# Sharing a ninth pair of attention weights, with a new order of steps in the second chunk and three roundings moved to ScalarE

## The chip, the core and the metric

The kernel runs on one core of a Trainium2 chip. The metric is the device time of one execution in microseconds (us); of several executions the median is given. The engines are TensorE (PE in the profile; PEld is its weight load), VectorE (DVE), ScalarE (ACT), GpSimd (POOL) and SyncE (SP), which issues most DMAs.

## The reference

Two stages are computed. The first is an attention without softmax, for 8 batches of 2496 tokens with keys and queries from the same array z (64 wide) and values v (256 wide):

```python
scores = scale * np.matmul(z, z.transpose(0, 2, 1))
attn = np.maximum(scores, 0.0) ** 2
out = np.matmul(attn, v)
return (u * out).astype(np.float32)
```

The second is a mixture of 8 experts over the 19968 rows that come out: a gate picks the expert of each row, a skip score leaves some rows as they are, and each expert is relu(x w1) w2. The weights attn are symmetric, since queries and keys are the same z: the weight of query i on key j is that of query j on key i. The change touches the attention stage alone.

## The kernel before, in words

**Tiling.** A batch's queries are cut into five chunks c = 0 to 4 (the first four of 512 queries, the fifth of 448). The keys are cut into ten steps p = 0 to 9 of 256 keys; steps 2j and 2j+1 cover the tokens of chunk j. All 40 chunks of the 8 batches follow one another in one written order, 400 steps in all. `ORDER[c]` says in which order a chunk takes its ten steps; a place in that order is called a position, 0 to 9. The first chunk of the first batch goes in plain order.

**A step's weights.** All products are made in three parts, from high and low halves of float32 numbers: the tile `ah` is the weight rounded to the float32r type, `al` is what is left. `scores` (line 263) makes six matmuls into PSUM (two run side by side on half the rows of the array, so they come in three pairs). ScalarE applies Relu (line 304) and Square (line 305) into a tile `r`. Line 327 rounds `r` to `ah`, on ScalarE or on VectorE as `on_act` says. VectorE subtracts to get `al` (line 331).

**Shared weights.** For a pair (i, j) of `PAIRS`, chunk i computes the weights of its steps 2j and 2j+1 and keeps them: `keep` (line 280) transposes each with two VectorE instructions into a tile `rt`, and after both steps four DMAs put it into DRAM (`kept`, line 292 reads it and line 705 issues the puts). Chunk j later does not compute its steps 2i and 2i+1 but recalls them, with four DMAs a step (`recall`). A recalled step has no scores, no Relu and no Square. In the fifth chunk, which is narrower, a recalled step is rounded and subtracted in three pieces. In the first batch the pairs with chunk 0 are not used.

**Where roundings run.** `on_act` gives a step's rounding to ScalarE if the step belongs to a pair or stands in `EXTRA[c]`, to VectorE otherwise.

**The order of one step s** (the loop over `steps`, `k` is the position). First `ahead` issues the recall of step s + 5 on SP. Then `stage` prepares the weights of step s + 2: scores, Relu, Square, rounding, subtraction, and the transposes of `keep`. Then `attend` multiplies the weights of step s with the values: 12 matmuls for each half d of the 256 outputs (line 358). Within the 12, the ninth is the first that needs `al`. At position 0 only d = 0 is done; at position 1 d = 0, then d = 1 of positions 0 and 1; at position 8 only d = 0; at position 9 d = 0, then d = 1 of positions 8 and 9. Then come the step's other jobs, by the table `todo`: loads of the next batch's z and v and their roundings, the transposed result rows (`rows0`, `rows1`, line 395), stores, and, during every second chunk, the routing of the last two chunks (`gates` on TensorE at position 1; `route`, `counts` on VectorE at position 3; `place` at position 5). Last, `put_some` issues up to four waiting puts on SP.

**The end of a chunk.** At position 9 the sums leave PSUM: `part(0, 1)` is a copy on ScalarE (line 386) and `part(0, 0)` an addition on VectorE (line 388), both after d = 0; `part(1, 1)` and `part(1, 0)` come after d = 1. The rounding and subtraction of the next chunk's position 0 are held back to here:

```python
high, low = rest
if s + 1 < len(steps) and not on_act(*steps[s + 1]):
    high()
    low()
    high = low = lambda: None
part(0, 1, acc[0])
part(0, 0, acc[0])
high()
low()
high, low = stage(s + LA)
```

So a rounding on VectorE comes before the copies, one on ScalarE behind the first copy. The rounding of the next chunk's position 1, if that step is not recalled, stands behind the copy `part(1, 1)` of the chunk's last sums, and its subtraction behind the chunk's last addition, `part(1, 0)`. Every engine runs its instructions in the written order.

**Buffers.** Two PSUM tiles for scores, five tiles `r` (recalls and computed steps share them), three each of `ah` and `al`, two of `rt`.

Of the kernel before, what the change touches and what calls it, by code (L numbers as in the profile page):

```python
# [25 lines left out]

PAIRS = ((0, 1), (0, 2), (0, 3), (1, 2), (1, 3), (2, 3), (2, 4), (3, 4))
ORDER = (  # L30
# [5 lines left out]
)  # L36
EXTRA = ((8,), (3, 8), (4, 5), (6, 7), (1, 3))


C_TRI, C_REV, C_OFF, C_IDS, C_THR, C_END = 0, 128, 192, 256, 260, 270  # L40
# [7 lines left out]
def attn_moe(ctx, tc, zT, uT, v, wg, w1, w2, cst, pad, out):  # L48
# [168 lines left out]
    def pairs(b):  # L217

        return PAIRS if b else [x for x in PAIRS if x[0]]

# [4 lines left out]
    def on_act(ci, p):  # L225
        b, c = ci // NQ, ci % NQ
        j = p // 2
        if (b, c) == (0, 0):
            return p in (4, 6)
        return (j, c) in pairs(b) or (c, j) in pairs(b) or p in EXTRA[c]  # L230

    kept = {x: dram.tile([QC, QC], F32, name="kept%d%d" % x) for x in PAIRS}
    HALF = (slice(0, 64), slice(64, 128))
# [796 lines left out]
```

## Time and profile before

| what | value |
|---|---|
| time, median of 3 runs (lowest, highest) | 1773.52 us (1771.78, 1775.19) |
| the profiled execution: its time, its span | 1774.26 us, 1772.5 us |
| TensorE matmuls | busy 1751.5 us, 99% of the span |
| TensorE weight loads | busy 1571.7 us, 89% |
| VectorE | busy 1196.0 us, 67% |
| ScalarE | busy 1159.2 us, 65% |
| DMA | 267.47 MB, mean 151 GB/s |

The span runs from the first to the last instruction; the time of an execution contains some 1.8 us around it. Matmuls overlap in the records, so a TensorE that is busy all the time need not be at its peak: what shows its pace is the distance from one matmul's start to the next. The attention stage ends at about 1275 us; the experts follow.

### The profile page before, as it was taken

To read this page: it belongs to the slowest core of one execution; us is meant where nothing else is said; L and a number is where in the kernel's file an instruction comes from. 1 tells how busy PE (TensorE), PEld (TensorE's weight loads), DVE (VectorE), ACT (ScalarE), POOL (GpSimd) and SP (SyncE) were. 2 spreads that over 40 slices of the span, in tenths; PEclk is the share of its full clock that TensorE was granted. 3 is DMA by queue.
4 is the path that set the end of the run, shared out by engine and by line. 5 is a ranking of instruction groups with operands and counts; after the bars stand their busy time and mean duration, and the time that the engine had idled before them with its cause. 6 is when DMAs were issued, how large, how long until landed. Compare 5 with 4: busy or idle time off the path is not lost. (4 is left out here: it accounts for less than half of the span.)

```text
span 1772.5 us, 40706 instructions
## 1 busy us (share of the span) xinstructions
PE 1751.5 (99%) x15844; PEld 1571.7 (89%) x15844; DVE 1196.0 (67%) x2113; ACT 1159.2 (65%) x1499; POOL 491.4 (28%) x483
## 2 busy tenths in 40 slices
PE   8999999999999999999999999999999999999998
PEld 6879888988888898888889888888899999999998
DVE  6878877887887787788778778867753333343332
ACT  8878877887788788778778877877533323333321
POOL 1102212211220221221122022112355546635721
PEclk9999999999999999999999999999999999999999
DMA  5576689478858947885794789579543323323210
GB/s 191 126 186 147 162 212 226 103 197 219 175 141 203 226 108 195 219 201 134 185 219 114 195 211 206 119 193 217 146 112 88 82 80 110 92 54 93 87 38 27
DMA packets 403766, 267.47 MB, mean 151 GB/s; under 512 B 205859, under 2 KB 334117, under 8 KB 403440
## 3 DMA queue, kind: packets, MB, share of 16 engines
q1 hardware_dynamic: 389440, 240.47, 55.6%
q0 software_dynamic: 13712, 22.99, 4.6%
q8 instruction: 142, 2.33, 0.6%
q14 instruction: 184, 1.51, 0.3%
q10 hardware_dynamic: 288, 0.17, 0.0%
HBM read 145.80 MB, written 118.39 MB: 149 GB/s over the span
## 5 line engine op out<-in xcount | busy, mean ns | idle before, releaser
L358 PE MATMUL acc<-ah,vh 64*128 64x512 f32 (+1 forms) x3120 | 654.6, 383 | 1.2 <-DVE ah L327 0.6
L358 PE MATMUL acc<-ah,vl 64*128 64x512 f32 (+1 forms) x3120 | 638.0, 382 | 0.0
L331 DVE TENSOR_TENSOR al<-r,ah 128x1024 fp32r<-128x1024 f32 (+3 forms) x464 | 488.4, 1068 | 185.2 <-ACT ah L327 175.4
L358 PE MATMUL acc<-al,vh 64*128 64x512 f32 (+1 forms) x3120 | 506.3, 383 | 2.2 <-DVE al L331 1.6
L517 POOL DMA_INDIRECT lst<-pair,dest x160 | 197.2, 1233 | 911.7 <-DVE dest L515 875.9
L304 ACT ACTIVATE r<-ps 128x1024 f32<-128x1024 f32 (+1 forms) x278 | 279.9, 1007 | 167.7 <-PE ps L263 158.7
L358 PEld LDWEIGHTS acc<-ah,vh 64*128 64x128 f32 x3120 | 344.6, 184 | 50.7 <-ACT ah L327 3.5
L358 PEld LDWEIGHTS acc<-ah,vl 64*128 64x128 f32 x3120 | 343.3, 184 | 41.3 <-DVE vl L120 0.3
L358 PEld LDWEIGHTS acc<-al,vh 64*128 64x128 f32 x3120 | 320.5, 184 | 53.0 <-DVE al L331 11.7
L327 ACT CAST ah<-r 128x1024 fp32r<-128x1024 f32 (+3 forms) x381 | 330.6, 892 | 55.5 <-PE acc L358 35.4
L305 ACT ACTIVATE r<-r 128x1024 f32<-128x1024 f32 (+1 forms) x278 | 290.0, 1043 | 8.8
L622 ACT ACTIVATE hh<-psh 128x512 fp32r<-128x512 f32 (+1 forms) x172 | 99.1, 584 | 287.9 <-PE psh L617 249.4
L617 PE MATMUL psh<-xt,w1h 128*128 128x256 f32 (+1 forms) x1280 | 235.3, 285 | 2.0 <-ACT xt L588 1.4
L636 PE MATMUL y<-w2t,hh 128*128 128x256 f32 x1328 | 235.5, 280 | 0.0
L623 DVE SCALAR_TENSOR_TENSOR hl<-psh,hh 128x512 fp32r<-128x512 f32 (+1 forms) x172 | 113.3, 671 | 137.5 <-ACT hh L622 134.6
L636 PEld LDWEIGHTS y<-w2t,hh 128*128 128x128 f32 x1328 | 201.8, 188 | 1.0 <-issue 0.6
L617 PEld LDWEIGHTS psh<-xt,w1h 128*128 128x128 f32 x1280 | 197.4, 189 | 2.9 <-issue 2.9
L636 PE MATMUL y<-w2t,hl 128*128 128x256 f32 x664 | 184.5, 278 | 1.3 <-DVE hl L623 1.3
L617 PE MATMUL psh<-xt,w1l 128*128 128x256 f32 (+1 forms) x640 | 182.1, 285 | 0.5 <-issue 0.5
L280 DVE STREAM_TRANSPOSE rt<-r 128x512 f32<-128x512 f32 x244 | 158.3, 686 | 0.7 <-DMA kept<-rt 0.5
L636 PEld LDWEIGHTS y<-w2t,hl 128*128 128x128 f32 x664 | 124.7, 188 | 1.7 <-DVE hl L623 1.7
L666 POOL DMA_INDIRECT out<-o,idt x77 | 76.7, 996 | 171.4 <-DVE o L665 148.6
(178 smaller groups left out, 1694.9 us busy)
## 6 DMA issues: line engine op xcount, KB each, us to landing
kept<-rt SPq DMA_DIRECT2D x244, 256.0 KB, 4.7
r<-kept SPq DMA_DIRECT2D x488, 128.0 KB, 4.5
raw<-in_v SPq DMA_DIRECT2D x80, 256.0 KB, 4.4
ut<-in_uT SPq DMA_DIRECT2D x32, 512.0 KB, 4.6
xr<-xrow SPq DMA_DIRECT2D x128, 128.0 KB, 3.2
out<-xrow SPq DMA_DIRECT2D x128, 128.0 KB, 3.0
raw<-in_w SPq DMA_DIRECT2D x64, 256.0 KB, 3.7
zf<-in_zT SPq DMA_DIRECT2D x40, 256.0 KB, 4.9
```

The lines of the kernel that those rows point to most:

```text
L280: nc.vector.transpose(t[:, :, 32 * k : 32 * k + 32], r[:, x, :].rearrange("p (m i) -> p m i", i=32))
L304: nc.scalar.activation(r[:, :, :n], ps[:, :, :n], AF.Relu, scale=isc)
L305: nc.scalar.activation(r[:, :, :n], r[:, :, :n], AF.Square)
L327: (nc.scalar.copy if on_act(ci, p) else nc.vector.tensor_copy)(h_, r_)
L331: nc.vector.tensor_sub(l_, r_, f32(h_))
L358: nc.tensor.matmul(acc[t][:, :n], w[h, x, dd], a[h, x, :n], start=(first and t not in halves[:m]), stop=(last and t not in halves[m + 1 :]),)
L517: put = nc.gpsimd.indirect_dma_start(out=lst, out_offset=bass.IndirectOffsetOnAxis(ap=dest[:, t : t + 1], axis=0), in_=pair[:, t, :], in_o ...
L617: nc.tensor.matmul(ps[:, j * W : (j + 1) * W], wt[:, a, o : o + P], x[:, d, :W], start=(m == 0), stop=(m == 5),)
L622: nc.scalar.activation(hh[:, : G * W], ps[:, : G * W], AF.Relu)
L623: nc.vector.scalar_tensor_tensor(hl[:, : G * W], ps[:, : G * W], 0.0, f32(hh[:, : G * W]), op0=ALU.max, op1=ALU.subtract)
L636: nc.tensor.matmul(ys[t], h[:, tt], w2t[f][:, k, :], start=(f == 0 and m == 0 and t % 2 == 0), stop=(f == NF - 1 and m == 2), skip_group_c ...
L666: put = nc.gpsimd.indirect_dma_start(out=out, out_offset=bass.IndirectOffsetOnAxis(ap=ids[:, t, 0:1], axis=0), in_=ot, in_offset=None, bou ...
```

## The change

A ninth pair, (1, 4), is added: the second chunk keeps its weights of steps 8 and 9, and the fifth chunk recalls its steps 2 and 3 from them. The second chunk takes its steps in a new order. `EXTRA` changes for the second and the fifth chunk. In the second chunk step 8 leaves the list, but as part of a pair it stays on ScalarE, and step 9 joins it there. In the fifth chunk steps 0, 2 and 8 move from VectorE to ScalarE (steps 0 and 8 by the list, step 2 as part of the pair), steps 1 and 3 stay on ScalarE, and only step 9 is left on VectorE.

```diff
-PAIRS = ((0, 1), (0, 2), (0, 3), (1, 2), (1, 3), (2, 3), (2, 4), (3, 4))
+PAIRS = ((0, 1), (0, 2), (0, 3), (1, 2), (1, 3), (1, 4), (2, 3), (2, 4), (3, 4))
 ORDER = (
     (0, 1, 2, 3, 8, 4, 5, 6, 7, 9),
-    (2, 3, 0, 4, 1, 5, 8, 6, 7, 9),
+    (2, 4, 5, 0, 6, 7, 1, 8, 9, 3),
     (4, 0, 1, 6, 2, 7, 3, 8, 9, 5),
     (6, 0, 2, 1, 8, 3, 9, 4, 5, 7),
     (0, 1, 2, 3, 4, 5, 6, 7, 8, 9),
 )
-EXTRA = ((8,), (3, 8), (4, 5), (6, 7), (1, 3))
+EXTRA = ((8,), (3,), (4, 5), (6, 7), (0, 1, 8))
```

In the new order of the second chunk, steps 0 and 1 are recalled at positions 3 and 6 (before: 2 and 4). Steps 4 to 9 are kept, at positions 1, 2, 4, 5, 7 and 8 (before: steps 4 to 7 at positions 3, 5, 7 and 8).

## The prediction

> **What bounds the kernel now.** First the page's busy times, then the chunks one by one, then the borders instruction by instruction.
>
> ```profile
> span 1772.5 us, 40706 instructions
> PE 1751.5 (99%) x15844; PEld 1571.7 (89%) x15844; DVE 1196.0 (67%) x2113; ACT 1159.2 (65%) x1499; POOL 491.4 (28%) x483
> PEclk9999999999999999999999999999999999999999
> ```
>
> TensorE is busy throughout at full clock. Busy time by windows, of the fifth batch: the second chunk (with a routing in it), the fourth, the fifth (without), and the fourth batch's fifth (with) (columns: window, length, busy PE, PEld, DVE, ACT, POOL with counts, clock, DMA share, GB/s).
>
> ```profile
> 677.35:710.44 33.09, 33.09 (x315) 27.01 (x313) 26.92 (x56) 26.82 (x31) 4.05 (x4) 1.00 0.76 185
> 741.24:774.19 32.95, 32.63 (x306) 26.24 (x308) 26.57 (x52) 22.87 (x28) 5.28 (x4) 1.00 0.89 225
> 774.19:801.78 27.59, 27.59 (x272) 25.70 (x270) 23.25 (x36) 21.77 (x35) 6.33 (x8) 1.00 0.73 157
> 615.67:644.69 29.02, 29.02 (x308) 27.65 (x306) 26.00 (x61) 21.94 (x37) 4.85 (x4) 1.00 0.66 156
> ```
>
> Every chunk is TensorE's: matmul time removed shortens it, unless a weight comes late and TensorE stands. ScalarE and VectorE are 70% to 90% busy, so whether one comes late is settled at places, not on the average. The place that decides is the border from fourth to fifth chunk (fifth batch; timeline of ScalarE, VectorE, TensorE):
>
> ```profile
> 771.99 0.95 ACT L305 ACTIVATE r<-r 128x896 f32<-128x896 f32 x1
> 773.79 0.59 ACT L386 COPY xrow<-acc 128x512 f32<-128x512 f32 x1 [0.84 <-PE acc L358]
> 774.27 0.94 ACT L327 CAST ah<-r 128x896 fp32r<-128x896 f32 x1
> 774.41 0.69 DVE L388 TENSOR_TENSOR xrow<-acc,xrow 128x512 f32<-128x512 f32 x1 [1.79 <-ACT xrow L386]
> 775.25 1.09 DVE L331 TENSOR_TENSOR al<-r,ah 128x896 fp32r<-128x896 f32 x1 [0.15 <-ACT ah L327]
> 773.13 0.62 PE L358 MATMUL acc<-al,vh 64*128 64x512 f32 x4
> 773.58 0.36 PE L263 MATMUL ps<-zh 64*128 64x448 f32 x2
> 774.19 0.36 PE L358 MATMUL acc<-ah,vh 64*128 64x448 f32 x2
> 775.00 0.57 PE L358 MATMUL acc<-al,vh 64*128 64x448 f32 x4
> 775.41 0.36 PE L263 MATMUL ps<-zh 64*128 64x448 f32 x2
> 776.02 0.36 PE L358 MATMUL acc<-ah,vh 64*128 64x448 f32 x2
> 776.82 0.57 PE L358 MATMUL acc<-al,vh 64*128 64x448 f32 x4
> ```
>
> The old chunk's last matmul issues before 773.58; its sums are copied from 773.79; behind the copy position 1's rounding runs to 775.21 and its subtraction to 776.34. TensorE meanwhile does step 2's scores (773.58 to 774.19), position 0 (to 775.41), step 3's scores (to 776.02), and starts position 1 at 776.02, needing `al` at 776.82. Both arrive in time, by 0.81 and 0.48 us.
>
> **The change part by part.** *Scores removed.* The two sets of scores just named are what the ninth pair takes away: 0.61 us each (774.19 - 773.58; 776.02 - 775.41), 1.22 us a batch, 9.8 us over eight. They are also the cover of that rounding.
>
> *What the cover hid.* Without them position 0 starts at 773.58 and is through after 1.22 us (775.41 - 774.19), at 774.80. The copy cannot start earlier, as the last sums are no earlier; so `ah` still ends at 775.21, `al` at 776.34. (Position 0's rounding now also sits on ScalarE behind the first copy and pushes the Relu and Square by 0.94 us, but the Square, which ended at 772.94, then ends near 773.8, when the copy starts anyway.) What a late weight costs TensorE, the border of the fourth chunk shows already:
>
> ```profile
> 740.14 2.00 ACT L327 CAST ah<-r 128x1024 fp32r<-128x1024 f32 x2
> 741.22 2.36 DVE L331 TENSOR_TENSOR al<-r,ah 128x1024 fp32r<-128x1024 f32 x2 [0.26 <-ACT ah L327]
> 741.24 0.50 PE L358 MATMUL acc<-ah,vh 64*128 64x512 f32 x2
> 741.58 0.39 PE L358 MATMUL acc<-ah,vl 64*128 64x512 f32 x2
> 742.50 0.73 PE L358 MATMUL acc<-al,vh 64*128 64x512 f32 x4
> ```
>
> TensorE starts 0.05 us after the first of the two casts ends (741.19), 0.05 us again after the subtraction that ends at 742.45 (the first of two, 1.23 us), and after each stand the next pair comes 0.11 us later than usual (0.34 us instead of 0.23; four matmuls of `al` in 0.73 us instead of the 0.62 of the row at 773.13). So in the changed fifth chunk position 1 starts at 775.26, 0.46 us late; its `al` is wanted 0.80 us on (776.82 - 776.02), at 776.06, and usable at 776.39: 0.33 more; restarts 2 x 0.11. Together 1.0 us. The fifth chunk gains 1.22 - 1.0 = 0.2 us, 1.6 us over eight batches. Bounds of the stall: nothing, if that rounding gets ahead of the copy, up to the whole 1.22.
>
> *Rest of the fifth chunk.* ScalarE loses two Relus and two Squares, VectorE three roundings; recalled steps pay more for their pieces. From position 2 on each step is recalled as positions 4 to 7 are now, and these run without a stand (27.59 us busy of 27.59), so I charge nothing; the cover is TensorE's 2.43 us a step (twice 1.22).
>
> *Second chunk.* Its count of computed and recalled steps is unchanged, so TensorE's work is. VectorE gets four transposes more and one rounding less.
>
> ```profile
> L280 DVE STREAM_TRANSPOSE rt<-r 128x512 f32<-128x512 f32 x244 | 158.3, 686 | 0.7 <-DMA kept<-rt 0.5
> L327 DVE CAST ah<-r 128x1024 fp32r<-128x1024 f32 x51 | 36.6, 718 | 17.7 <-ACT r L305 17.5
> ```
>
> 4 x 0.686 - 0.718 = 2.0 us more in 33.09, of which 26.92 are busy. ScalarE gets that rounding. It fits on average; the tight place is position 6 where a routing runs (VectorE, then TensorE, batch 5):
>
> ```profile
> 691.90 1.23 DVE L331 TENSOR_TENSOR al<-r,ah 128x1024 fp32r<-128x1024 f32 x1 [2.84 <-ACT ah L327]
> 693.05 1.30 DVE L280 STREAM_TRANSPOSE rt<-r 128x512 f32<-128x512 f32 x2
> 694.27 0.18 DVE L459 TENSOR_REDUCE mx<-lg 128x8 f32<-128x64 f32 x1
> 697.69 0.69 DVE L120 TENSOR_TENSOR vl<-raw,vh 128x512 fp32r<-128x512 f32 x1
> 698.29 2.35 DVE L331 TENSOR_TENSOR al<-r,ah 128x1024 fp32r<-128x1024 f32 x2
> 698.84 0.40 PE L358 MATMUL acc<-ah,vh 64*128 64x512 f32 x2
> 699.76 0.62 PE L358 MATMUL acc<-al,vh 64*128 64x512 f32 x4
> ```
>
> From 691.90 VectorE runs without a gap: position 5's subtraction, its transposes, the routing, the load's remainder, then position 6's subtraction, which ends near 699.5, a quarter of a microsecond before the 699.76 at which TensorE wants it. Scores for position k + 2 run at the start of position k: up to position 6 that is at positions 1, 3, 4, 5, 6 in the old order, at 0, 2, 3, 5, 6 in the new. So position 5's scores, made at position 3, stand behind two sets instead of one, and its Relu with the whole train behind it comes one set, 0.68 us, later (three pairs, each half of 773.58 - 773.13). Position 6 stands behind five sets either way: its need is no later, and it is now the recalled step 1. VectorE's gap of 2.84 us ahead of the train takes up the transposes that moved before it. `al` comes near 700.2, 0.45 us late, plus 0.11 to restart: 0.56 us. Chunks alternate, so four of eight second chunks have a routing: 2.2 us. Without the routing's 3.4 us (694.27 to 697.69) nothing is late. Bounds: 0 if the train's slack is larger than I read, 1.0 us a chunk if the added transposes of positions 1 and 2 push it too.
>
> *DMAs.* The pair adds four puts, which wait on SP for VectorE's transposes with recalls and stores behind them; the second chunk's DMA share is 0.76, and the puts of steps 4 to 7 now go out earlier, so I charge nothing. The moved recalls are wanted later than before. It adds eight recalls of 128 KB, 1.05 MB, to the busiest stretch:
>
> ```profile
> 768.75 2.46 SPq L292 DMA_DIRECT2D r<-kept  x4
> 779.34 2.98 SPq L292 DMA_DIRECT2D r<-kept  x4
> 777.00:780.00 3.00, 3.00 (x32) 2.78 (x32) 2.35 (x5) 2.94 (x5) 1.87 (x2) 1.00 1.05 240
> r<-kept SPq DMA_DIRECT2D x488, 128.0 KB, 4.5
> 793.04 0.37 PE L358 MATMUL acc<-ah,vh 64*128 64x448 f32 x2
> L331 DVE TENSOR_TENSOR al<-r,ah 128x384 fp32r<-128x384 f32 x64 | 39.5, 657 | 2.5 <-ACT ah L327 2.4
> ```
>
> The new ones stand on SP just ahead of the first row. The last old one is issued by 782.3 and lands 4.5 us on, at 786.8; position 7, which uses it, starts at 793.04 and wants `al` 0.8 us later, with at most 3 us for the pieces' rounding and subtraction before: the data has until 790.8, 4.0 us of slack. 1.05 MB at 240 GB/s is 4.4 us if DMA engines, at a share of 1.05 here, give everything back one to one. SP is ahead of TensorE, so I take part of it as hidden, cost 0; the other bound is 0.6 us a batch and more if transfers lengthen.
>
> By the Trainium skill's "Perfetto Trace Analysis", section Identifying the Most-Contended Engine, a DMA share misleads and use of the HBM is to be read instead; with the roughly 358 GB/s limit of "DMA: Bandwidth & Descriptors", section Specifications, 240 leaves room, 1.05 MB would be an estimated 2.9 us, inside the slack. No run here shows that rate; the trace has shares of 1.0 at 240.
>
> *The sum.* -9.8 + 8 x 1.0 + 2.2 = +0.4 us on the profiled execution's 1774.26, so 1774.7. That execution lies 0.7 us above the median shown, 1773.52: on the median 1773.9, and I predict 1774.
>
> **The rivals.**
>
> *The cover isn't needed: faster.* If position 1's rounding is not what TensorE waits for in the fifth chunk, the 8.0 us of stalls are saved: 1774 - 8 = 1766. For: today both arrive with 0.5 us to spare. Against: copy, rounding and subtraction follow one another, whatever else is removed.
>
> *The recalls come late: slower.* A full DMA stretch delays the fifth chunk's last recalls. It decides above 4.0 us of delay; at 4.8 us, 0.8 us a batch, 6.4 us in all: 1780. For: the share above 1. Against: only the last two recalls are near their limit.
>
> *TensorE has room: no change, a little slower.* The weight loads fill 25.70 of the fifth chunk's 27.59 us; if the remaining 1.89 us were idle time, 1.22 us of removed scores would buy nothing and only the second chunk's 2.2 us stay: 1776. Against: matmul pairs start every 0.20 us (775.00 to 775.41 for two), without a gap. The skill's section named above judges TensorE's headroom by weight loads and would read it so; this trace's even spacing speaks against it.
>
> *The change doesn't do what it says.* All three roundings do leave VectorE (0, 2 and 8), and the recalled steps exist; no weight on this.
>
> **How the numbers follow.** Forecast 0.53, faster rival 0.23, late recalls 0.19, room on TensorE 0.05. The forecast's own range is 1770.5 to 1777. From the rivals the range goes to 1765.5 and 1780, which leaves about 0.15 out. This kernel's measurement tells 0.2%, 3.5 us, from no change. Faster by more: 0.24 (the first rival, and a sliver of the forecast). Slower by more: 0.20 (late recalls, a sliver likewise). Within: 0.56.
>
> **What would show it.** In the fifth chunk: twelve score matmuls fewer, and a stand of TensorE at position 1 of about 1 us, released by ScalarE's `ah` and VectorE's `al`; the chunk 0.2 us shorter. If it is 1.2 us shorter, the cover was not needed. In second chunks with routing: a stand at position 6 near 0.5 us, released by `al`. If ScalarE waits for `r` from DMA there, the late recalls hold. A stall at a place not named here would make the prediction wrong as worked.

## The result, and the profile after

The changed kernel takes 1802.03 us (median of 4 runs, 1800.55 to 1807.37); the kernel before, run beside it, 1774.3 us. The ratio is 1.0167, with an interval of 1.0155 to 1.0179: slower by 30 us by the ratio, where 1774 us (no change) was forecast. The profiled execution is the slowest of the four (1807.37 us), so sums over its trace come out some 5 us larger than the medians would give. The page after, busy times and one row of its DMA issues (count, size, median us to landing):

```profile
span 1805.5 us, 40756 instructions
PE 1761.0 (98%) x15748; PEld 1541.1 (85%) x15748; DVE 1199.2 (66%) x2145; ACT 1161.5 (64%) x1531; POOL 503.7 (28%) x483
r<-kept SPq DMA_DIRECT2D x552, 128.0 KB, 4.8
```

96 matmuls fewer (15844 before), 64 recalls more (488 before): the change does what it says. The same windows as in the prediction (fourth batch's fifth chunk with a routing; of the fifth batch the second, the fourth and the fifth):

```profile
628.40:662.90 34.50, 30.55 (x303) 25.32 (x300) 25.36 (x63) 21.18 (x40) 5.46 (x4) 1.00 0.77 187
696.22:729.13 32.91, 32.58 (x308) 26.05 (x306) 28.34 (x59) 27.24 (x31) 5.30 (x4) 1.00 0.82 203
760.23:792.56 32.33, 32.02 (x301) 25.51 (x302) 26.01 (x51) 23.02 (x28) 5.94 (x4) 1.00 0.90 215
792.56:823.96 31.40, 29.32 (x267) 24.44 (x264) 22.34 (x38) 20.76 (x38) 7.56 (x9) 1.00 0.81 187
```

The second and fourth chunks are a little shorter in these windows. (A window begins at the chunk's first product with values; a set of scores of the second chunk falls into the first chunk's window now, and the fourth chunk's has lost one of the two sets that the pair removes.) The fifth chunks are where the time goes: 29.02 to 34.50 us and 27.59 to 31.40 us, though each has a set of scores less. TensorE is idle for 2.1 us of the last row's 31.40 (31.40 - 29.32); in the prediction's rows the fifth chunks had no idle time. The DMA engines are as full as they were: over the first 20 us of this chunk, in which the recalls land, their share is 0.99 at 230 GB/s, where the same stretch before (774.19 to 794.19) has 1.00 at 216.

The predicted stand at the border is there. Timeline of the fifth batch's border (start, us, engine, instruction, idle time and its releaser):

```profile
792.76 0.59 ACT L386 COPY xrow<-acc 128x512 f32<-128x512 f32 x1
793.25 0.94 ACT L327 CAST ah<-r 128x896 fp32r<-128x896 f32 x1
794.22 1.09 DVE L331 TENSOR_TENSOR al<-r,ah 128x896 fp32r<-128x896 f32 x1
794.24 0.47 PE L358 MATMUL acc<-ah,vh 64*128 64x448 f32 x2 [0.31 <-ACT ah L327]
795.37 0.67 PE L358 MATMUL acc<-al,vh 64*128 64x448 f32 x4
```

Position 1's first pair starts 0.67 us after the pair ahead (0.20 is the pace), the first pair of `al` 0.42 us after its own, and the pair behind each comes another 0.11 us late: about 0.9 us together. But this is the smaller part. Adding up over the eight fifth chunks by how much the distance from one pair's start to the next is above 0.20 us gives 7.0 us at position 1, 10.5 us at positions 2 to 7, 3.5 us at position 8 and 13.4 us at position 9. (At the end of two of these chunks TensorE ran at half its clock for 3.41 us, as the last section shows; the wider spacing there is about 1.5 us of the sum at position 8.) The waits of ScalarE, first in the kernel before, then after (what waits, for what: us in total, times, longest), name the cause:

```profile
ACT ah L327 <- DMA r<-kept: 6.7, 7, 3.4
```

```profile
ACT ah L327 <- DMA r<-kept: 73.7, 44, 3.0
```

ScalarE waits for recalled weights, 44 times instead of 7. Timeline of SP in the fifth chunk of the fifth batch (DMAs issued; a row ends when the last of them is issued):

```profile
793.50 3.09 SPq L292 DMA_DIRECT2D r<-kept  x4
796.85 0.35 SPq L103 DMA_DIRECT2D zf<-in_zT  x1
797.30 2.50 SPq L292 DMA_DIRECT2D r<-kept  x4
800.09 0.35 SPq L95 DMA_DIRECT2D raw<-in_v  x1
800.63 2.53 SPq L292 DMA_DIRECT2D r<-kept  x4
803.54 0.35 SPq L103 DMA_DIRECT2D zf<-in_zT  x1
804.03 3.04 SPq L292 DMA_DIRECT2D r<-kept  x4
807.12 0.43 SPq L95 DMA_DIRECT2D raw<-in_v  x1
```

SP goes from one issue to the next almost without a break. From 793.50 to 804.03 it needs 10.5 us for three steps of four recalls and a load: 3.5 us a step, 0.70 us a DMA. TensorE asks for a step every 2.43 us. The issues themselves take only 5.1 of the 10.5 us (0.30 to 0.42 us each); the rest is waiting between them. What SP waits for while it issues recalls, before and after:

```profile
SPq L292 <- DVE al L331: 21.3, 16, 2.8
SPq L292 <- DMA r<-kept: 11.1, 14, 1.9
```

```profile
SPq L292 <- DMA r<-kept: 21.9, 51, 2.5
SPq L292 <- DMA raw<-in_v: 14.9, 18, 2.7
```

Before, its longest wait was for VectorE to free a tile `r`, the sign of a queue that is ahead; after, that wait is down to 2.1 us. All its waits at recalls for DMAs to land come to 36 us before and 58 us after. SP's DMAs go through eight semaphores in turn: of the 693 DMAs in the trace of after that have a record of their landing, none was followed, eight DMAs later, by one issued before that landing, and 128 by one issued within 0.15 us of it (50 of 484 before). Eight in flight at the 4.8 us of the page's row is one every 0.6 us.

Last, what the late recall does to ScalarE and TensorE (same chunk):

```profile
811.41 1.13 ACT L327 CAST ah<-r 128x384 fp32r<-128x384 f32 x3 [1.76 <-DMA r<-kept]
812.96 0.91 ACT L304 ACTIVATE r<-ps 128x896 f32<-128x896 f32 x1
816.26 0.91 ACT L304 ACTIVATE r<-ps 128x896 f32<-128x896 f32 x1
```

```profile
818.87 0.47 PE L358 MATMUL acc<-ah,vh 64*128 64x448 f32 x2 [1.19 <-DVE ah L327]
820.06 0.67 PE L358 MATMUL acc<-al,vh 64*128 64x448 f32 x3 [0.32 <-DVE al L331]
```

ScalarE stands until 811.41 for step 7's recall. The Relus of steps 8 and 9 are behind that rounding on ScalarE, so they come late too, and TensorE has its longest stand of this chunk, 1.19 us, at position 9, whose weights are computed and not recalled.

### The profile page after: what moved, and what is told of

The parts are those of the page before. It is cut to its first block, busy times and chain, and to the rows that moved or that the text cites. A ratio compares the mean times of both kernels' runs of the same rounds, so it can differ in the third digit from the quotient of the medians.

```text
span 1805.5 us, 40756 instructions
## 1 busy us (share of the span) xinstructions
PE 1761.0 (98%) x15748; PEld 1541.1 (85%) x15748; DVE 1199.2 (66%) x2145; ACT 1161.5 (64%) x1531; POOL 503.7 (28%) x483
## 4 chain that ended last, share of the span: by engine, by line
PE 65%; DMA 14%; ACT 8%; DVE 6%; SPq 3%; issue 3%; POOL 0%; DVEq 0%; POOLq 0%; ACTq 0%
PE acc L358 35%; PE psh L617 11%; PE y L636 10%; PE ps L263 7%; DMA r<-kept 7%; DVE al L331 3%; ACT ah L327 2%; ACT r L305 2%; SPq L292 2%; ACT r L304 2%; DMA out<-o,idt 2%; DMA zf<-in_zT 2%; DMA xr<-xrow 1%; DMA raw<-in_v 1%; DVE rt L280 1%
## 5 line engine op out<-in xcount | busy, mean ns | idle before, releaser
L358 PE MATMUL acc<-ah,vh 64*128 64x512 f32 (+1 forms) x3120 | 638.1, 386 | 15.4 <-DVE ah L327 7.7
L358 PE MATMUL acc<-ah,vl 64*128 64x512 f32 (+1 forms) x3120 | 620.3, 382 | 0.0
L358 PE MATMUL acc<-al,vh 64*128 64x512 f32 (+1 forms) x3120 | 495.1, 386 | 8.3 <-DVE al L331 7.0
L327 ACT CAST ah<-r 128x1024 fp32r<-128x1024 f32 (+3 forms) x445 | 364.4, 847 | 126.6 <-DMA r<-kept 73.7
L358 PEld LDWEIGHTS acc<-ah,vh 64*128 64x128 f32 x3120 | 319.2, 184 | 79.7 <-ACT ah L327 18.6
L358 PEld LDWEIGHTS acc<-al,vh 64*128 64x128 f32 x3120 | 301.6, 184 | 74.7 <-DVE al L331 29.0
L358 PEld LDWEIGHTS acc<-ah,vl 64*128 64x128 f32 x3120 | 319.3, 185 | 46.4 <-DVE vl L120 0.3
L304 ACT ACTIVATE r<-ps 128x1024 f32<-128x1024 f32 (+1 forms) x262 | 265.3, 1012 | 131.1 <-PE ps L263 122.8
L305 ACT ACTIVATE r<-r 128x1024 f32<-128x1024 f32 (+1 forms) x262 | 274.7, 1049 | 8.3
L280 DVE STREAM_TRANSPOSE rt<-r 128x512 f32<-128x512 f32 x276 | 179.1, 687 | 0.6 <-DMA kept<-rt 0.5
```

The lines of the kernel that those rows point to most:

```text
L280: nc.vector.transpose(t[:, :, 32 * k : 32 * k + 32], r[:, x, :].rearrange("p (m i) -> p m i", i=32))
L304: nc.scalar.activation(r[:, :, :n], ps[:, :, :n], AF.Relu, scale=isc)
L305: nc.scalar.activation(r[:, :, :n], r[:, :, :n], AF.Square)
L327: (nc.scalar.copy if on_act(ci, p) else nc.vector.tensor_copy)(h_, r_)
L358: nc.tensor.matmul(acc[t][:, :n], w[h, x, dd], a[h, x, :n], start=(first and t not in halves[:m]), stop=(last and t not in halves[m + 1 :]),)
```

## The experiments

Theory: the recalls come late because SP can't issue them fast enough, having only eight DMAs in flight (the program's eight semaphores). Rivals: the added bytes (DMA engines or memory full); the border's order; the roundings on ScalarE; the new order of the second chunk. Every ratio is against the kernel before, run beside the experiment, since the kernel before itself took between 1773 and 1787 us from one chip to another; a time in an expectation is to be read as its ratio to 1774.

**The parts without the ninth pair.** `e1_order`: the kernel before with the new order of the second chunk. `e2_round`: the kernel before with the fifth chunk's roundings of the kernel after.

```diff
-    (2, 3, 0, 4, 1, 5, 8, 6, 7, 9),
+    (2, 4, 5, 0, 6, 7, 1, 8, 9, 3),
```

```diff
-EXTRA = ((8,), (3, 8), (4, 5), (6, 7), (1, 3))
+EXTRA = ((8,), (3, 8), (4, 5), (6, 7), (0, 1, 2, 3, 8))
```

Expected of `e1_order`:

> The kernel before with the new order of the second chunk alone (no ninth pair, the roundings as before). By the prediction's step: one late subtraction at position 6 in four chunks, 0.56 us each: 1776 to 1777. If the order costs nothing: 1774. If the order is what costs: above 1785.

Expected of `e2_round`:

> The kernel before with the fifth chunk's steps 0, 2 and 8 rounded on ScalarE, as in the change, and nothing else. Late recalls (theory): no recall is late, the roundings have cover, 1773 to 1777. Rival, the roundings on ScalarE cost: above 1785.

Measured: 1.0018 (1.0009 to 1.0028) and 1.0010 (0.9998 to 1.0022): 3 us and 2 us, so neither part explains the 30. As far as the parts add up, the pair itself brings the rest.

**More DMAs on the kernel before.** Eight extra DRAM-to-DRAM DMAs a batch at the place of the new recalls, of 128 KB (`e9_bytes`) or of 4 KB (`e10_slots`). Nothing uses what they write.

```diff
+            if ci % NQ == 4 and p in (2, 3):
+                d = dram.tile([8, 32, 2, QC], F32, name="dum%d" % s)
+                src = kept[2, 4].rearrange("(a k i) q -> a i k q", a=4, k=4)
+                for a in range(4):
+                    nc.sync.dma_start(d[4 * (p - 2) + a], src[a, :, p % 2 * 2 : p % 2 * 2 + 2, :])
```

(`e10_slots` takes `:16` of the last dimension on both sides.)

Expected of `e9_bytes`:

> The kernel before with eight DMAs more a batch, at the places in SP's order where the change puts the eight new recalls: 128 KB each, from the kept weights to an unused place in DRAM; nobody waits for them and nothing else is changed, the scores are still made. Late recalls: the four old recalled steps now come late by about 4 to 5 us less the 4.0 us of slack and the 1.2 us that the scores still take, so 1775 to 1790, with ScalarE waiting for r from DMA. Rivals (roundings, order, lost cover): 1774.

Expected of `e10_slots`:

> As the run with eight extra DMAs of 128 KB, but of 4 KB each (64-byte runs): they take places among SP's eight in flight but hardly any bytes. If places are what is short, it costs at least half of what the 128 KB ones cost; if bytes, nothing: 1774.

Measured: 1.0117 (1.010 to 1.0134) and 1.0108 (1.0085 to 1.013). A thirty-second of the bytes, nearly the same time. ScalarE's wait in each:

```profile
ACT ah L327 <- DMA r<-kept: 62.5, 33, 4.1
```

```profile
ACT ah L327 <- DMA r<-kept: 45.3, 26, 3.7
```

And SP with the 4 KB DMAs:

```profile
778.26 6.31 SPq L714 DMA_DIRECT2D dum<-kept  x8
```

0.79 us for each 4 KB: the bytes don't count here. (A DMA of 4 KB has as many separate runs, 64, as one of 128 KB, so the number of runs is left as a rival; `e17_one` below, with the runs of a step unchanged, settles it.) With no scores taken away, the kernel before loses some 20 us to eight DMAs a batch.

**The same bytes in fewer DMAs.** `e6_two` recalls a step with two DMAs of 256 KB over all 128 partitions; the DRAM side's outermost step is the four blocks `a`.

```diff
-        src = kept[p // 2, ci % NQ].rearrange("(a k i) q -> a i k q", a=4, k=4)
-        for a in range(4):
-            nc.sync.dma_start(r[32 * a : 32 * a + 32], src[a, :, p % 2 * 2 : p % 2 * 2 + 2, :])
+        src = kept[p // 2, ci % NQ].rearrange("(a k i) q -> k a i q", a=4, k=4)
+        for x in range(2):
+            nc.sync.dma_start(r[:, x, :], src[p % 2 * 2 + x])
```

Expected of `e6_two`:

> The changed kernel with every recall made by two DMAs of 256 KB instead of four of 128 KB; the bytes are the same. If the recalls are late because SP has no more than eight DMAs in flight (each DMA waits for the one eight before it): half as many places taken by recalls, 1774 to 1785. If they are late because the DMA engines are full of bytes: unchanged, 1797 to 1806, the 256 KB landing about twice as late as the 128 KB (9 us instead of 4.8).

Measured: 1.1912, ScalarE waiting for recalls nearly everywhere:

```profile
ACT ah L327 <- DMA r<-kept: 463.8, 156, 6.3
```

That is far from any answer of the expectation. By the Trainium skill's "DMA: Bandwidth & Descriptors", section Why a DMA increments its semaphore by 16 and not by 1, a DMA uses the largest number of engines, up to 16, that divides the slowest dimension of both sides, here 4; no view shows the engines one by one, so the cause isn't shown, and the run says nothing on the number of DMAs.

`e17_one` therefore changes the layout in DRAM: `keep` writes its 32-row blocks in another order, so that the 128 partitions of a recall are evenly spaced, and one DMA of 512 KB brings a step.

```diff
-            nc.vector.transpose(t[:, :, 32 * k : 32 * k + 32], r[:, x, :].rearrange("p (m i) -> p m i", i=32))
+            nc.vector.transpose(
+                t[:, :, 32 * k : 32 * k + 32].rearrange("p (k a) i -> p k a i", k=4),
+                r[:, x, :].rearrange("p (a k i) -> p k a i", a=4, k=4),
+            )
...
-        for a in range(4):
-            nc.sync.dma_start(r[32 * a : 32 * a + 32], src[a, :, p % 2 * 2 : p % 2 * 2 + 2, :])
+        src = kept[p // 2, ci % NQ].rearrange("(k e) q -> e k q", k=4)
+        nc.sync.dma_start(r, src[:, p % 2 * 2 : p % 2 * 2 + 2, :])
```

Expected of `e17_one`:

> The changed kernel with the kept weights laid out in DRAM so that a recalled step comes with one DMA of 512 KB instead of four of 128 KB; the bytes are the same. If the number of DMAs in flight (eight from SP, each about 5 us) is what delays the recalls, the fifth chunk's late recalls go and only the stand at its position 1 (1.0 us) is left: ratio 0.999 to 1.004. If the bytes (DMA engines or HBM full at 240 GB/s) delay them, the recalls stay late and the ratio stays at 1.012 to 1.018.

Measured: 1.0006 (0.9997 to 1.0016). Its page, its fifth chunk of the fifth batch, ScalarE's wait, and SP's largest wait at the recalls (line 294 here):

```profile
r<-kept SPq DMA_DIRECT2D x138, 512.0 KB, 6.6
```

```profile
775.70:803.57 27.87, 27.51 (x266) 24.81 (x264) 22.14 (x38) 20.87 (x38) 7.70 (x8) 1.00 0.68 184
```

```profile
ACT ah L329 <- DMA r<-kept: 0.7, 1, 0.7
```

```profile
SPq L294 <- DVE al L333: 63.6, 38, 3.5
```

Each DMA takes longer to land (6.6 us against 4.8) and moves four times as much. A step still consists of 256 runs of 2 KB. The chunk moves its bytes at 184 GB/s, as in the slow kernel (187), and its first 20 us at 256 GB/s against 230; yet no recall of a fifth chunk is late, and SP is ahead again: it waits for free tiles, and at the recalls not once for a landing. TensorE has one stand left, the one at position 1:

```profile
777.38 0.47 PE L360 MATMUL acc<-ah,vh 64*128 64x448 f32 x2 [0.31 <-ACT ah L329]
```

With `e9_bytes` and `e10_slots`: neither the bytes nor the number of runs is the cause, but the number of DMAs; and the late recalls cost 1.0167 - 1.0006, or 1.6%: 28.5 us, 3.6 us a batch, good to some 3 us by the two intervals. `e20_b_one` gives the kernel before the same recall:

Expected of `e20_b_one`:

> The kernel before (eight pairs, its own order and roundings), with one DMA of 512 KB a recalled step. In the kernel before no recall comes late at a fifth chunk, so if late recalls are all that the DMAs cost, it gains nothing: ratio 0.998 to 1.002. If fewer DMAs make the kernel faster in themselves, it comes to 0.997 or below, and the gain of the ninth pair with one DMA a step is not the pair's.

Measured: 1.001 (1.0001 to 1.002), as expected. It gains nothing where nothing was late.

**Other ways around the lateness.** `e5_late`: the kernel after, with the last six loads of the next batch begun behind the recalls.

```diff
-            jobs += [(load_v, 7, 4, 2), (load_z, 2, 4, 3), (load_v, 8, 4, 4), (load_z, 3, 4, 5)]
-            jobs += [(load_v, 9, 4, 6), (load_z, 4, 4, 7)]
+            jobs += [(load_z, 4, 4, 8), (load_v, 8, 4, 9), (load_z, 2, 4, 10), (load_v, 7, 4, 11)]
+            jobs += [(load_z, 3, 4, 12), (load_v, 9, 4, 13)]
```

Expected of `e5_late`:

> The changed kernel with the last six loads of the next batch (z and v) begun some four to six steps later, behind the fifth chunk's recalls. Late recalls: the recalls no longer share the queue with them and land in time; of the 33 us that fifth chunks grew by, only the stand at position 1 stays (about 1.0 us a batch), so 1774 to 1782. Rivals that lay it to the roundings, the order or the lost cover alone: unchanged within 4 us, 1798 to 1806.

Measured: 1.0068 (1.0051 to 1.0084), more than the 1.000 to 1.005 expected. The fifth chunks keep little but the stand at position 1 (7.1 us over the eight, and 1.5 us at positions 3 and 4 of three of them), and the first chunks, into which the loads' casts move, become 0.7 us longer each, which I hadn't priced. In the kernel after, too, the last fifth chunk, with no next batch to load, stands for 1.1 us by the sum above, the other seven for 3.8 to 5.5. Loads and recalls share SP's eight places, so fewer loads among the recalls help them as fewer DMAs a recall do.

`e3_dve`: the kernel after with steps 0 and 8 of the fifth chunk rounded on VectorE (`EXTRA[4]` is `(1,)`).

Expected of `e3_dve`:

> The changed kernel with the fifth chunk's steps 0 and 8 rounded on VectorE again. Late recalls (theory): the fifth chunk's recalls still land late, since no DMA is changed; only the knock-on at position 9 shrinks, because ScalarE has 0.94 us less to do between the late step 7 and step 9's Relu. At most 0.9 us a batch, so 1795 to 1801 us. Rival, the roundings on ScalarE are what costs: back to 1775 to 1780.

Measured: 1.0133 (1.0115 to 1.015), some 6 us less than the kernel after and within what was expected. The recalls stay as late (ScalarE waits 43 times for them, 87.9 us), but the stand at position 9 shrinks, from 1.19 to 0.46 us in the fifth batch:

```profile
808.73 0.47 PE L358 MATMUL acc<-ah,vh 64*128 64x448 f32 x2 [0.46 <-DVE ah L327]
```

Over all fifth chunks the sum at position 9 falls from 13.4 to 9.3 us. This is the part that passes through ScalarE's order: one rounding less ahead of step 9's Relu.

`e11_pool` issues the recalls of steps 2 and 3 from GpSimd's queue instead of SP's.

```diff
+            eng = nc.gpsimd if ci % NQ == 4 and p in (2, 3) else nc.sync
-            nc.sync.dma_start(r[32 * a : 32 * a + 32], src[a, :, p % 2 * 2 : p % 2 * 2 + 2, :])
+            eng.dma_start(r[32 * a : 32 * a + 32], src[a, :, p % 2 * 2 : p % 2 * 2 + 2, :])
```

Expected of `e11_pool`:

> The changed kernel with the eight new recalls (the fifth chunk's steps 2 and 3) issued on GpSimd's queue instead of SP's; bytes, times and readers are the same. If SP's places in flight are what is short, SP's queue is as it was before: only the stand at position 1 stays, 1774 to 1782. If bytes are short: unchanged, 1797 to 1806.

Measured: 1.0197 (1.018 to 1.0214), slower still, as neither answer had it. The fifth batch's step 3, and the clock behind it:

```profile
789.58 2.25 POOL L293 DMA_DIRECT2D r<-kept  x4
800.08 2.15 ACT L328 CAST ah<-r 128x384 fp32r<-128x384 f32 x6 [5.93 <-DMA r<-kept]
801.26 0.65 PE L359 MATMUL acc<-ah,vh 64*128 64x448 f32 x2 [4.35 <-ACT ah L328]
```

```profile
801.26:804.50 3.24, 3.24 (x18) 2.95 (x20) 3.24 (x9) 3.03 (x8) 1.99 (x2) 0.52 1.06 234
```

These recalls, all issued by 791.83, had landed only when ScalarE could start at 800.08, so the run doesn't test the places on SP. After the stand of 4.35 us TensorE ran at a granted clock of 0.52.

**The border.** `e18_swap`: the kernel after with steps 1 and 2 of the fifth chunk exchanged, so that a recalled step, whose rounding can run ahead of the copy, is at position 1. `e15_swap_late` adds the late loads of `e5_late`, `e19_swap_one` instead the recall of `e17_one`. `e7_inter` goes further and puts computed steps among all the recalled ones.

```diff
-    (0, 1, 2, 3, 4, 5, 6, 7, 8, 9),
+    (0, 2, 1, 3, 4, 5, 6, 7, 8, 9),
```

`e7_inter` has `(0, 2, 1, 3, 8, 4, 5, 9, 6, 7)` there.

Expected of `e18_swap`:

> The changed kernel with the exchange of steps 1 and 2 in the fifth chunk alone. The stand at position 1 goes, the recalls stay late: both theories expect 1.0167 less 0.45%, 1.010 to 1.014. If it falls to 1.000 or below, the stand at position 1 was what made the recalls late.

Expected of `e15_swap_late`:

> The changed kernel with four DMAs a recall, the exchange of steps 1 and 2 in the fifth chunk, and the last six loads of the next batch moved behind the recalls. The late loads alone left the stand of 1.0 us in the fifth chunk and 0.7 us more in the first chunk, ratio 1.007. The exchange takes the 1.0 us away: eight times, 8 us, 0.45%: ratio 1.001 to 1.004.

Expected of `e19_swap_one` ("the one above" is `e17_one`):

> The one above, and in the fifth chunk step 2 (recalled) at position 1 and step 1 (computed) at position 2. The copy of the last sums then no longer stands ahead of position 1's rounding, so that the 1.0 us stand goes too: the 9.8 us of removed scores stay, less 2.2 us at the second chunk: ratio 0.995 to 0.998 if the number of DMAs is the cause, 1.008 to 1.014 if the bytes are.

Expected of `e7_inter`:

> The changed kernel with the fifth chunk in the order 0, 2, 1, 3, 8, 4, 5, 9, 6, 7: the six recalled steps are spread over nine positions and one of them sits at position 1. The DMAs are the same in number and bytes over the chunk. Late recalls because six in a row ask for 24 DMAs faster than SP's eight places give them: mostly cured, and the stand at position 1 (1.0 us a batch) with it, 1766 to 1778. If the DMA engines lack bandwidth over the chunk: 1790 or more.

Measured: `e18_swap` 1.0178 (1.0161 to 1.0195), no better than the kernel after, against my expectation. `e15_swap_late` 1.0017 (1.0005 to 1.0029), `e19_swap_one` 0.9971 (0.9961 to 0.9982), `e7_inter` 1.0072 (1.0046 to 1.0097), where 0.996 to 1.002 was expected. In the trace of `e18_swap` the stand at position 1 is gone, but the recalls are as late as after (ScalarE waits 43 times for them, 78.5 us): with late recalls the time is the same; that the wait has only moved is argued. Where they aren't late it gains 0.5% (`e5_late` to `e15_swap_late`) and 0.35% (`e17_one` to `e19_swap_one`), 6 to 9 us, near the 8.0 us that I gave position 1. The computed steps among the recalled ones (`e7_inter`) give SP time, so that ScalarE waits less for recalls than after, but not all of the lateness goes:

```profile
ACT ah L327 <- DMA r<-kept: 51.5, 28, 6.5
```

The fifth chunk of `e19_swap_one` runs without a stand, 0.61 us shorter than before (27.59):

```profile
771.15:798.13 26.98, 26.98 (x266) 24.97 (x264) 21.62 (x37) 21.36 (x36) 6.23 (x8) 1.00 0.63 175
```

`e13_inter_pool` joins `e7_inter` and `e11_pool`:

Expected of `e13_inter_pool`:

> Both: the spread order of the fifth chunk and the eight new recalls on GpSimd's queue. If late recalls and the stand at position 1 are the whole loss, what is left is 9.8 us of scores saved less 2.2 us in the second chunk: 1766, at most 1772. If something else costs too: above 1775.

Measured: 1.0233 (1.0216 to 1.025). ScalarE waits up to 9.0 us for a recall; with the recalls from GpSimd's queue as late as that, this run too tells nothing of SP.

**The second chunk.** `e4_oldorder` is the kernel after with the old order of the second chunk, `e12_pairorder` one with `(2, 3, 0, 4, 1, 5, 6, 7, 8, 9)`. Both steps of a pair are turned into the one tile `rt` of the chunk, one after the other. In `e4_oldorder` steps 8 and 9 stand around 6 and 7. In `e12_pairorder` the written order is right, but the kernel puts off the transposes of position 8 until behind those of position 9 (lines 334 and 789), so that step 9's come before step 8's. In both, the kept weights are a mixture of steps of two pairs: this part of the computation is changed.

Expected of `e4_oldorder`:

> The changed kernel with the old order of the second chunk (the ninth pair and the roundings stay). Late recalls: the new order costs only its stand at position 6 in the four second chunks with a routing, 0.56 us each, so about 2 us less, 1798 to 1801. Rival, the new order upsets the second chunk and what follows: under 1785.

Expected of `e12_pairorder`:

> The changed kernel with the second chunk in the order 2, 3, 0, 4, 1, 5, 6, 7, 8, 9: the old one, with step 8 moved behind 7, so that the two kept steps 8 and 9 follow one another as the ninth pair's tile needs. Late recalls: this takes away only the stand at position 6 in routed second chunks, 0.56 us in four chunks: 1798 to 1802. If the new order is to blame: under 1785.

Measured: 1.0278 (1.026 to 1.0297) and 1.0273 (1.0251 to 1.0295), outside both answers. Since the dependencies of the transposes and puts change with it, neither says what the order costs; `e1_order` does.

`e21_swap_one_load` is `e19_swap_one` with one load begun a position later, so that its remainder on VectorE (line 120) is no longer ahead of position 6's subtraction.

```diff
-            jobs = [(load_v, 0, 1, 3), (load_z, 0, 1, 6), (load_v, 1, 2, 3), (load_z, 1, 2, 5), (load_v, 2, 2, 7)]
+            jobs = [(load_v, 0, 1, 4), (load_z, 0, 1, 6), (load_v, 1, 2, 3), (load_z, 1, 2, 5), (load_v, 2, 2, 7)]
```

Expected of `e21_swap_one_load`:

> The changed kernel with one DMA a recalled step, steps 1 and 2 of the fifth chunk exchanged, and one load of the next batch's values begun a position later in the second chunk, so that its remainder on VectorE (0.69 us) comes behind the subtraction of position 6. If this remainder is what makes the stand at position 6 of the second chunk with a routing, these four chunks become 0.5 to 0.7 us shorter each: 2 to 3 us, ratio 0.9971 less 0.0014, 0.995 to 0.997. If the stand comes from the transposes, 0.997 stays.

Measured: 0.9954 (0.994 to 0.9967), 1763.94 us: faster than the kernel before by 8 us. The fifth batch's second chunk in `e19_swap_one` and here:

```profile
674.81:708.09 33.28, 32.57 (x309) 25.84 (x306) 28.35 (x59) 27.23 (x31) 5.31 (x4) 1.00 0.81 208
```

```profile
674.42:707.14 32.72, 32.58 (x308) 25.84 (x306) 28.29 (x59) 27.00 (x31) 4.74 (x4) 1.00 0.80 210
```

0.56 us less, all of it idle time of TensorE (0.71 to 0.14 us). Three second chunks became shorter, those of the third, fifth and seventh batch, by 0.54 to 0.60 us: 1.7 us, and the ratio fell by 3 us, which the intervals allow.

## Why the prediction was wrong, step by step

**Scores removed, -9.8 us: right.** In `e19_swap_one` the fifth batch's fifth chunk is 0.61 us shorter than before; the other set lay in the fourth chunk (32.95 before, 32.33 after).

**What the cover hid, +8.0 us: right.** About 0.9 us where 1.0 was worked out (7.0 us over the eight chunks). Position 1 started 0.47 us late, where 0.46 was forecast; the second stand was 0.22 us and not 0.33, as the first restart had already moved the products of `al` by 0.11 us, which my sum counted twice. The first rival (cover not needed) falls with it: where nothing else is late, as in `e17_one`, this stand is what is left. (The fifth chunk's window there is 0.28 us longer than before, 27.87 against 27.59, and not 0.2 us shorter, because one of the two removed sets lay in the fourth chunk's window.)

**Second chunk, +2.2 us: right in place, and in size for one chunk; one chunk too many.** TensorE's stand there after, released by `al` as forecast:

```profile
718.34 0.73 PE L358 MATMUL acc<-al,vh 64*128 64x512 f32 x4 [0.34 <-DVE al L331]
```

The pair comes 0.50 us later than the pace of 0.23 and the next 0.11: 0.61 us against 0.56. But it stands so in three chunks and not four, 1.8 us: the first batch's second chunk, which recalls nothing, takes 34.31 us before and after. `e1_order` alone costs 3.2 us (1.6 to 5.0). `e21_swap_one_load` shows that the load's remainder is one of the instructions that hold the subtraction up.

**Rest of the fifth chunk, 0: wrong as put.** "These run without a stand, so I charge nothing" took four recalled steps in a row as the measure of six. In `e17_one` and `e19_swap_one` they do run without one, so ScalarE and VectorE have the room; it was the data that came late.

**DMAs, "SP is ahead of TensorE, so I take part of it as hidden, cost 0; the other bound is 0.6 us a batch": this is the step that failed.** It measured 3.6 us a batch, 28.5 us in all. (The bound itself isn't worked out in the text: 4.4 us of transfer less 4.0 of slack are 0.4.) Three things went wrong in it.

First, I took SP to be ahead and asked for bytes. My own rows say that four recalls take SP 2.46 and 2.98 us; beside the 2.43 us of a step this leaves SP no time for the loads. Before, with only four recalled steps in a row, SP could live on a lead; with six the lead is used up. (That there was a lead is argued from SP's waits for free tiles; `e10_slots` shows that eight more DMAs a batch were too many for it.) The rate to compare was DMAs per step, not GB/s. The Trainium skill's rule on the use of the memory ("Perfetto Trace Analysis", Identifying the Most-Contended Engine) isn't contradicted: the bytes fit, by `e17_one` with 184 GB/s. It was only not the limit. The Trainium skill's same page, section What "DMA-bound" means, also says that an issuing sequencer filled with DMA slices is a limit of its own, which I didn't weigh; it calls such time the making of descriptors, while here half of it is waiting between the issues (5.4 of 10.5 us above), for landings among other things, by SP's waits.

Second, the slack was read at one place. I gave the last recall 4.0 us of slack and at most 4.8 us of delay. It landed 18.6 us after the fourth chunk's end (811.2 - 792.56), where I had 13.2 (786.8 - 773.58): 5.4 us of delay, so size and threshold were close. But I priced only what it does to position 7. The recalls of steps 4 to 6 were late as well: 10.5 us at positions 2 to 7.

Third, I let the lateness end with the recalled steps. ScalarE runs in order, and steps 8 and 9 are computed behind the late rounding: 3.5 + 13.4 = 16.9 us at positions 8 and 9 (1.5 of it the half clock), the largest term, and nowhere in my text. That it passes through ScalarE's order is shown for some 6 us of it, by `e3_dve`; the rest is read from the timeline.

**The rivals.** "The recalls come late" was the right mechanism, and the sign named for it (ScalarE waits for `r`) is there, but it had a chance of 0.19 and a price of 6.4 us instead of 28.5. "TensorE has room" falls with the fifth chunk of `e19_swap_one`, 0.61 us shorter by the very scores removed.

The sum without the failed step, +0.4 us, a ratio of 1.0002, is what `e17_one` measured: 1.0006 (0.9997 to 1.0016). That it fits so well is partly luck: the stands at position 1 came out some 0.9 us smaller than my term, and the first batch's first chunk, which my sum doesn't touch, takes 35.65 us there instead of 34.38, for a reason not looked into.

## What to carry to other kernels

Ask of an issuing queue what you ask of an engine: count its DMAs per step of the bounding engine, times the time that each takes there (here four to five times 0.6 to 0.7 us against 2.43), and see in its waits whether it waits for free tiles (it is ahead) or for landings (it is behind). Fewer and larger DMAs can buy that room without a byte saved, as in `e17_one`; that the shape matters too shows in `e6_two`. And follow a late input past the instruction that needs it: on an engine that runs in order, everything written behind it is late as well, and a repair elsewhere (the exchange at the border) gains nothing until the lateness is gone.

## What I hadn't expected of the hardware

- A DMA of 4 KB held SP's queue as long as one of 128 KB (0.79 and 0.70 us each where the queue was full), while 512 KB landed in 6.6 us against 4.8 us for 128 KB.
- Two DMAs of 256 KB in another shape were far slower than four of 128 KB: 1.1912.
- Recalls from GpSimd's queue were late by their own: step 3's in the fifth batch landed some 8.2 us after the last of its four was issued.
- While these kernels ran, TensorE's clock fell for 3.41 us at a time, or a multiple of it. The stand of 4.35 us in `e11_pool` was followed by more than 3 us at half the clock (0.52), but much shorter stands can do it too. In the kernel after the granted clock was 0.50 for 3.41 us at the end of the first and of the third batch's fifth chunk, and stayed 1.00 in the other fifth chunks, though similar stands are there. The two falls begin 324.26 us apart, 95 times 3.413. In the 3.41 us just ahead of each, TensorE was busy for 1.96 and 1.92 us; in the fifth batch's chunk, counted on from the falls in steps of 3.41 us, the stretch with the stand had 2.21 us and no fall behind it:

```profile
166.89:170.30 3.41, 1.96 (x14) 0.81 (x12) 2.67 (x5) 3.35 (x5) 0.00 (x0) 1.00 0.49 149
170.30:173.71 3.41, 3.31 (x17) 2.99 (x18) 3.10 (x5) 2.12 (x3) 0.00 (x0) 0.50 0.01 2
491.15:494.56 3.41, 1.92 (x14) 1.13 (x16) 2.68 (x4) 3.35 (x5) 0.00 (x0) 1.00 0.18 67
494.56:497.97 3.41, 3.41 (x22) 3.05 (x20) 2.54 (x4) 2.36 (x4) 0.00 (x0) 0.50 0.00 0
815.42:818.83 3.41, 2.21 (x18) 1.10 (x14) 2.32 (x3) 3.38 (x6) 0.00 (x0) 1.00 0.72 181
```

So it seems to be the work within such a stretch, and not the length of one stand, that decides, and where the stretches happen to begin; where the limit lies isn't shown. `e17_one`, `e19_swap_one` and the kernel before have no such fall before their last microseconds.
